# Top-32 attention with an MLP: which engine turns the softmax weights, and who takes the notes

## The chip, the core and the metric

The kernel runs on one core of one Trainium2 chip. The metric is the device time of one execution in microseconds (us). A core has five engines with a queue of instructions each: TensorE (PE in the profile; PEld is its weight load), VectorE (DVE), ScalarE (ACT), GpSimd (POOL) and SyncE (SP, which here only issues transfers). An engine takes its instructions in the order in which they were written; engines wait for one another through semaphores.

## The reference, cut to what matters

Eight batches of eight heads, 576 queries and keys, head size 64; all float32.

```python
scores = scale * np.matmul(q, k.transpose(0, 1, 3, 2))          # scale = 1/8
kth = np.partition(scores, -32, axis=-1)[..., -32:-31]
scores = np.where(scores >= kth, scores, -1e9)                  # the 32 largest of 576
attn = softmax(scores)                                          # shift by the max, divide by sum + 1e-9
x = np.matmul(attn, v)            # (8, 8, 576, 64), then heads side by side: (8, 576, 512)
xn = (x - mean) / np.sqrt(var + 1e-6) * g_ln                    # over the 512
out = x + np.maximum(xn @ w_ch1, 0) @ w_ch2                     # 512 -> 2048 -> 512
```

## The kernel before, in words

**Units.** A *job* is a pair of heads of one batch with a set of query tiles. The 576 queries are four tiles of 128 and a rest of 64. A *unit* is one such tile for both heads of the pair, so two score matrices of 128 x 576; the rest's unit holds both heads in one 128 x 576 matrix. There are 160 units, 32 of them rests. Queries of a job that share one value product are a *group*: batch 0 has groups of two tiles and rests by themselves, batch 1 groups [0, 1] and [2, 3, rest], batches 2 to 7 first [0, 1, rest] for four head pairs and then [2, 3] for four.

**A step.** The main loop has a step `n` for each unit, and the code writes each engine's order by hand (`tc.manual_schedule()`). A unit is worked on in several steps:

- TensorE makes its scores (line 386) one or two steps ahead, and ScalarE copies them into the tile `sc` (line 367; five buffers).
- VectorE selects in step `n`: `halve` (lines 407 and 408) makes pairwise maxima `hi` and minima `lo` (written one step ahead, `hi` has two buffers), and `select(u, 0..3)` finds the 32nd largest with MAX8 and MATCH_REPLACE8 (lines 429, 415, 421).
- `prepare` (lines 437 to 445) makes three small notes from the result: `watch` (line 452) notes how far the selection was from failing, line 444 makes `edge` (the threshold times a huge factor) and line 445 `bias` (the maximum times -scale). Each is 128 x 2 or 128 x 1. For the first 17 units VectorE does this at the end of the unit's own step, and from then on GpSimd (`CONVERTING`), in the next step.
- One step later ScalarE marks the dropped keys (`mask`, line 481, needs `edge`), GpSimd subtracts the scores (line 484), and two steps later ScalarE exponentiates into the tile `e` (`weigh`, line 492).
- The weights must then lie with keys on partitions, in the tile `pt` (one buffer), for the value product. TensorE turns them: `turn` transposes four blocks of 128 keys for each head (line 546) and one block with the last 64 keys of both heads (line 575); ScalarE copies each PSUM bank to `pt` (lines 558 and 576).
- For 72 *moved* units (batches 2 to 7; no rests, and not the last unit of a group) VectorE does most of it instead: `move` transposes 32 x 32 blocks of the first 512 keys of each head in two instructions (line 524) into the unit's spent `sc` tile, SyncE sends that to device memory (`turned`, line 529), and four more transfers (line 532) bring it back to `pt` with 32-row strips in the right places. The last 64 keys still go over TensorE. `move` stands at the end of the step, behind `select(u, 3)`.
- A step after a group's last unit was turned, `values` multiplies with the values (`av`, lines 600 and 607, at the beginning of the step), `take_values` and `place` bring the result into the rows of `x`.

**MLP.** When rows of `x` are complete, `stats` and a queue `todo` follow: hidden matmuls (line 745) and projections (lines 784 and 902), pieces of which `fill()` puts between the attention's instructions on TensorE. How much a step gets is a plan (`slot`, from `pe_cost` and `dve_cost`): up to step 17 the difference of the two costs, later an even share of what is left. SyncE's queue holds, in one order, the transfers of `move`, loads of heads and values, the forms of the second weight (line 971), denominators and outputs.

Of the kernel before, what the change touches and what calls it, by code (L numbers as in the profile page):

```python
# [10 lines left out]
ALU = mybir.AluOpType  # L11
FP32 = mybir.dt.float32
# [7 lines left out]
STEEP = 2.0**90  # L20
LN_EPS = 1.0e-6
J = 4
# [7 lines left out]
def compute(  # L30
# [12 lines left out]
    nc = tc.nc  # L43
    P = nc.NUM_PARTITIONS
    B, H, S, D = q.shape
# [3 lines left out]
    JP = J * P  # L49
    R = S - JP  # L50
    NHP = H // 2
# [9 lines left out]
    GQ = 2 * P + R  # L61
# [10 lines left out]
    ptpool = pool("pt", 1)  # L72
# [13 lines left out]
    hbmpool = pool("hbm", 4, space=bass.MemoryType.DRAM)  # L86
# [350 lines left out]
    def prepare(u):  # L437

        nt = len(u.tiles)
        u.bias, u.edge = u.thr[:, 0:nt, 5], u.thr[:, 0:nt, 6]  # L440
        if doubt is not None:
            watch(u)
        eng = nc.vector if u.i < CONVERTING else nc.gpsimd
        eng.tensor_scalar(u.edge, u.thr[:, 0:nt, 7], STEEP, 0.0, ALU.mult, ALU.add)  # L444
        eng.tensor_scalar(u.bias, u.top[:, 0:nt, 0], -scale, 0.0, ALU.mult, ALU.add)

    def watch(u):

        nt = len(u.tiles)
        c = 1 + 2 * (u.i % 16)  # L450
        eng = nc.vector if u.i < CONVERTING else nc.gpsimd
        eng.tensor_tensor(  # L452
            watched[:, c : c + nt], u.hi[:, 0:nt, HALF + 7], u.thr[:, 0:nt, 7], ALU.subtract
        )
        if u.i % 16 == 15 or u.i == N - 1:
            u.ends_watch = True
# [49 lines left out]
    def place_of(u):  # L506

        g = u.group  # L510
        if g.pt is None:
            g.pt = ptpool.tile([P, 2 * J + 1, GQ], FP32, tag="pt", name="pt")
            g.blocks = g.pt[:, 0 : 2 * J].rearrange("p c n -> p (c n)").rearrange(
                "p (i h c n) -> p h i c n", h=2, c=J, n=32
            )
        return sum(P for x in g.qts if x < u.qt) // 32

    def move(u):

        i0 = place_of(u)  # L520
        ni = P // 32
        blocks = u.sc[:].rearrange("p t n -> p (t n)")[:, 0 : 2 * JP]
        for t in range(2):
            nc.vector.transpose(
                blocks.rearrange("p (j t c n) -> p j t c n", j=ni, t=2, c=J)[:, :, t],
                u.e[:, t, t * R : t * R + JP].rearrange("p (c j k) -> p j c k", c=J, k=32),
            )
        hbm = hbmpool.tile([P, 2 * JP], FP32, tag="turned", name="turned")
        nc.sync.dma_start(hbm[:], blocks)
        for j in range(ni):  # L530
            to = u.group.pt[j * 32 : (j + 1) * 32, 0 : 2 * J].rearrange("k c n -> k (c n)")
            nc.sync.dma_start(
                to[:, i0 * 2 * P : (i0 + ni) * 2 * P].rearrange("k (i x) -> k i x", i=ni),
                hbm[:, j * 2 * P : (j + 1) * 2 * P].rearrange("(i k) x -> k i x", k=32),
            )

    def turn(u):

        g = u.group
        i0 = place_of(u)  # L540
        q0 = i0 * 32

        def part(t):
            ps = turned()
            for c in range(J):
                nc.tensor.transpose(  # L546
                    ps[:, c * P : (c + 1) * P], u.e[:, t, c * P + t * R : (c + 1) * P + t * R],
                    ident[:],
                )
            if u.rest:  # L550
                both = ps[:].rearrange("p (c h n) -> p h c n", h=2, n=R)
                for h in range(2):
                    nc.scalar.copy(
                        g.blocks[:, h, i0 : i0 + R // 32],
                        both[:, h].rearrange("p c (i n) -> p i c n", n=32),
                    )
            else:
                nc.scalar.copy(  # L558
                    g.blocks[:, t, i0 : i0 + P // 32],
                    ps[:].rearrange("p (c i n) -> p i c n", c=J, n=32),  # L560
                )

        def last():
            ps = turned()
            if u.rest:
                nc.tensor.transpose(ps[0:R, 0:P], u.e[:, 0, JP:S], ident[:])
                nc.tensor.transpose(ps[:, P : 2 * P], u.e[:, 0, JP - R : S], ident[:])
                for h in range(2):
                    nc.scalar.copy(
                        g.pt[h * R : (h + 1) * R, 2 * J, q0 : q0 + R],  # L570
                        ps[h * R : (h + 1) * R, h * (P + R) : h * (P + R) + R],
                    )
            else:
                ends = u.e[:].rearrange("p t n -> p (t n)")[:, JP : JP + P]
                nc.tensor.transpose(ps[:, 0:P], ends, ident[:])
                nc.scalar.copy(g.pt[:, 2 * J, q0 : q0 + P], ps[:, 0:P])

        heads = () if u.moved else range(len(u.tiles))
        return [lambda t=t: part(t) for t in heads] + [last]

    xs, xps, rs, oTr, dr = {}, {}, {}, {}, {}

# [12 lines left out]
    def values(g):  # L595
        vb = g.job.v
        av = brief("av")
        for c in range(J):
            for h in range(2):
                nc.tensor.matmul(  # L600
                    av[h * D : (h + 1) * D, 0 : g.nq],
                    vb[:, h * J + c, :],
                    g.blocks[:, h, 0 : g.nq // 32, c, :],
                    start=(c == 0),
                    stop=False,
                )
        nc.tensor.matmul(
            av[:, 0 : g.nq], g.job.ends[:], g.pt[:, 2 * J, 0 : g.nq],
            start=False, stop=True,
        )  # L610
        g.av = av
# [320 lines left out]
    blocks = []  # L932
# [59 lines left out]
    jobs = []  # L992
# [27 lines left out]
    CONVERTING = max(n for n in batches if batches[n]) + 2  # L1020
    EARLY = jobs[NHP].first

    for u in units[jobs[5 * NHP].first :]:
        u.moved = not u.rest and u is not u.group.units[-1]


    full = slice(0, P)
# [137 lines left out]
    load_gain()  # L1165
    weights(-1, 0)
    weights(-1, 1)
    for n in range(END):
        now[0] = n
        if n in gives:  # L1170
# [16 lines left out]
        moved = ex is not None and ex.moved  # L1187
# [27 lines left out]
        if ex and len(ex.tiles) > 1 and not early:  # L1215
            weigh(ex, 1)
        fill()
        if g:
            take_values(g)
        if parts and not moved:  # L1220
            parts[0]()
        if ex and ex.rest:
            keep_den(ex)
# [79 lines left out]
        if late and late.job.hp == NHP - 1:  # L1303
            r = late.job.b // 2
            if r % 2:
                for x in (r - 1, r):
                    arrived(n, ("r", x), rs[x])
        fill()
    while todo or any(x.waiting for x in (sums_later, ends_later, stores)):
        tick[0] += 1  # L1310
        stores.settle(2)
        ends_later.settle(1)
        sums_later.settle(1)
        fetch_forms(1)
        if todo:
            pop()
# [50 lines left out]
```

## Time and profile before

| | before |
|---|---|
| three runs | 1652.8, 1662.5, 1662.7 us (median 1662.5) |
| profiled execution | 1655.4 us, of it the profile's span 1653.6 us, mean granted clock 0.963 |
| TensorE busy | 1508.0 us (91%) |
| VectorE busy | 1334.3 us (81%) |
| ScalarE busy | 1067.4 us (65%) |
| GpSimd busy | 1078.1 us (65%) |
| transfers | 211.5 MB, 43.8% of the 16 DMA engines' span on the main queue |

"Busy" counts the time with at least one instruction running on the engine; the rest of the span is idle, and for idle time the profile names the instruction whose end released the engine ("<-"). A group's line has the kernel line, engine, operation, output and inputs, shapes and count, then its busy time, the mean duration of one, and the idle time ahead of it. PEclk is the clock that TensorE was granted, 1.00 at most. A matmul shows twice in the counts of float32 products (two passes); a transpose shows once.

### The profile page before, as it was taken

To read this page: it belongs to the slowest core of one execution; us is meant where nothing else is said; L and a number is where in the kernel's file an instruction comes from. 1 tells how busy PE (TensorE), PEld (TensorE's weight loads), DVE (VectorE), ACT (ScalarE), POOL (GpSimd) and SP (SyncE) were. 2 spreads that over 40 slices of the span, in tenths; PEclk is the share of its full clock that TensorE was granted. 3 is DMA by queue.
4 is the path that set the end of the run, shared out by engine and by line. 5 is a ranking of instruction groups with operands and counts; after the bars stand their busy time and mean duration, and the time that the engine had idled before them with its cause. 6 is when DMAs were issued, how large, how long until landed. Compare 5 with 4: busy or idle time off the path is not lost. (4 is left out here: it accounts for less than half of the span.)

```text
span 1653.6 us, 27426 instructions
## 1 busy us (share of the span) xinstructions
PE 1508.0 (91%) x7898; PEld 1132.7 (68%) x7898; DVE 1334.3 (81%) x3990; ACT 1067.4 (65%) x2712; POOL 1078.1 (65%) x1607
## 2 busy tenths in 40 slices
PE   2557898999989899899999999999989999999997
PEld 1235546677757677677777776677767777778886
DVE  6878998788989898899998988799879999884000
ACT  5777966677757676567666765677656766654311
POOL 4667866867657475667675866576756676856433
PEclk9768999999989999999999999999999999999999
DMA  7433434321454354554655444545554445442211
GB/s 199 110 100 114 130 81 119 114 66 46 109 167 152 109 168 118 162 153 118 185 160 168 126 126 135 163 138 138 158 158 150 134 135 181 149 131 71 91 32 53
DMA packets 358951, 211.52 MB, mean 128 GB/s; under 512 B 250756, under 2 KB 331144, under 8 KB 358792
## 3 DMA queue, kind: packets, MB, share of 16 engines
q1 hardware_dynamic: 354056, 209.10, 43.8%
q8 instruction: 65, 1.06, 0.3%
q10 hardware_dynamic: 4736, 0.59, 0.2%
q14 instruction: 94, 0.77, 0.2%
HBM read 145.62 MB, written 63.96 MB: 127 GB/s over the span
## 5 line engine op out<-in xcount | busy, mean ns | idle before, releaser
L484 POOL TENSOR_TENSOR e<-e,sc 128x576 f32<-128x576 f32 x288 | 412.4, 1435 | 419.4 <-ACT e L481 403.1
L745 PE MATMUL hps<-xT,w 128*128 128x256 f32 x2304 | 548.2, 384 | 2.5 <-ACT xT L707 2.5
L745 PEld LDWEIGHTS hps<-xT,w 128*128 128x128 f32 x2304 | 422.0, 191 | 72.8 <-issue 16.7
L429 DVE MAX8 m<-hi 128x8 f32<-128x296 f32 (+1 forms) x1152 | 464.3, 444 | 1.1
L415 DVE MATCH_REPLACE8 hi<-m,hi 128x288 f32<-128x288 f32 (+1 forms) x864 | 378.2, 444 | 0.0
L902 PE MATMUL ops<-w,h 128*128 128x256 f32 x1360 | 324.8, 381 | 0.0
L902 PEld LDWEIGHTS ops<-w,h 128*128 128x128 f32 x1360 | 247.7, 190 | 40.4 <-issue 6.9
L492 ACT ACTIVATE e<-e,m 128x576 f32<-128x576 f32 x288 | 224.8, 780 | 52.8 <-POOL e L484 52.4
L407 DVE TENSOR_TENSOR hi<-sc 128x576 f32<-128x576 f32 (+1 forms) x160 | 120.1, 751 | 157.4 <-POOL watched L452 135.7
L481 ACT ACTIVATE e<-sc,m 128x576 f32<-128x576 f32 x288 | 223.9, 781 | 14.6 <-POOL m L444 13.9
L367 ACT COPY sc<-scps 128x288 f32<-128x288 f32 x576 | 195.1, 406 | 38.6 <-PE scps L386 18.3
L600 PE MATMUL av<-pt,vb 128*64 128x256 f32 (+2 forms) x1088 | 159.4, 439 | 37.7 <-DMA pt<-turned 18.2
L768 ACT ACTIVATE h<-hps 128x512 f32<-128x512 f32 x144 | 86.5, 601 | 103.7 <-PE hps L745 102.9
L600 PEld LDWEIGHTS av<-pt,vb 128*64 128x64 f32 x1088 | 80.2, 149 | 106.5 <-issue 50.3
L386 PE MATMUL scps<-kT,late_qT 64*128 64x288 f32 (+3 forms) x832 | 129.0, 413 | 5.3 <-ACT pt L558 3.2
L902 PE MATMUL ops<-wt,s 128*128 128x256 f32 x544 | 129.2, 381 | 0.0
L546 PE MATMUL tp<-ident,e 128*128 128x128 f32 x576 | 93.9, 289 | 37.8 <-ACT e L492 37.4
L386 PE MATMUL scps<-kT,qT 64*128 64x288 f32 x512 | 94.8, 471 | 29.5 <-ACT sign L168 11.8
L408 DVE TENSOR_TENSOR lo<-sc 128x576 f32<-128x576 f32 (+1 forms) x160 | 120.9, 756 | 0.0
L546 PEld LDWEIGHTS tp<-ident,e 128*128 128x128 f32 x576 | 73.9, 148 | 65.7 <-ACT e L492 51.6
L421 DVE MAX8 hi<-lo 128x8 f32<-128x288 f32 x288 | 118.0, 446 | 0.0
L386 PEld LDWEIGHTS scps<-kT,late_qT 64*128 64x128 f32 (+1 forms) x832 | 72.0, 168 | 59.4 <-issue 23.5
(106 smaller groups left out, 1905.9 us busy)
## 6 DMA issues: line engine op xcount, KB each, us to landing
turned<-sc SPq DMA_DIRECT2D x72, 512.0 KB, 2.6
pt<-turned SPq DMA_DIRECT2D x288, 128.0 KB, 2.7
w<-forms SPq DMA_DIRECT2D x136, 256.0 KB, 3.8
vb<-in_v_dram SPq DMA_DIRECT2D x136, 128.0 KB, 3.1
raw<-in_moe_w_ch_dram SPq DMA_DIRECT2D x32, 512.0 KB, 4.3
kT<-kept SPq DMA_DIRECT2D x36, 288.0 KB, 3.2
kin<-in_k_dram SPq DMA_DIRECT2D x128, 72.0 KB, 2.3
kept<-kT SPq DMA_DIRECT2D x32, 288.0 KB, 2.9
```

The lines of the kernel that those rows point to most:

```text
L367: nc.scalar.copy(u.sc[:, t, s * HALF : (s + 1) * HALF], made[s][t][:, 0:HALF])
L386: nc.tensor.matmul(ps[i * R : i * R + ql, o : o + width], qT[r, q0 : q0 + ql], kT[r, k0 : k0 + width], start=True, stop=True,)
L408: nc.vector.tensor_tensor(lo, a, b, ALU.min)
L415: nc.vector.match_replace(x, m[:, t, :], x, LOWEST)
L429: nc.vector.max(m[:, t, :], u.hi[:, t, 0:width])
L481: nc.scalar.activation(u.e[:, t], u.sc[:, t], AF.Relu, bias=u.edge[:, t : t + 1], scale=-STEEP)
L484: nc.gpsimd.tensor_tensor(u.e[:, t], u.e[:, t], u.sc[:, t], ALU.subtract)
L492: nc.scalar.activation(u.e[:, t], u.e[:, t], AF.Exp, bias=u.bias[:, t : t + 1], scale=-scale, accum_out=g.den[:, col : col + 1],)
L546: nc.tensor.transpose(ps[:, c * P : (c + 1) * P], u.e[:, t, c * P + t * R : (c + 1) * P + t * R], ident[:],)
L600: nc.tensor.matmul(av[h * D : (h + 1) * D, 0 : g.nq], vb[:, h * J + c, :], g.blocks[:, h, 0 : g.nq // 32, c, :], start=(c == 0), stop=False,)
L745: nc.tensor.matmul(ps[0][:, side * N : (side + 1) * N], w1[:, c, f * P : (f + 1) * P], self.xT[:, c, 0:N], start=(c == 0), stop=(c == NC - 1),
L902: nc.tensor.matmul(bank[name][:, 0:Q], a(j), rhs, start=first and j == 0, stop=(j == G - 1), skip_group_check=not first,)
```

## The change

- 118 units are moved instead of 72: all from unit 8 to the last but one, except rests and unit 15. Last units of a group are now among them.
- `move` turns all 1152 columns (both heads' 576 keys) in one VectorE instruction. A moved unit has no `turn` any more: its transposes on TensorE and copies on ScalarE are gone, those of the last 64 keys too.
- `pt` is laid out by blocks of 32 queries with nine rows of blocks each (four of head 0, the shared last keys, four of head 1), so that the strips from device memory land in one run of 288 numbers.
- `move` stands ahead of `select(u, 2)` in the step instead of behind `select(u, 3)`.
- A group whose last unit is moved has its value product one half step to one step later, at the end of the step (`late_values`); the result is taken in the next step, and the MLP block that hangs on it is given a step later.
- `watch` and `edge` are made by VectorE for all units, in the unit's own step behind `select(u, 3)`; `bias` stays with GpSimd from unit 17 on, written in the same place. 
- The plan counts a moved unit 0.0 instead of 0.15 for TensorE.

```diff
@@ prepare, watch
         if doubt is not None:
             watch(u)
+        nc.vector.tensor_scalar(u.edge, u.thr[:, 0:nt, 7], STEEP, 0.0, ALU.mult, ALU.add)
         eng = nc.vector if u.i < CONVERTING else nc.gpsimd
-        eng.tensor_scalar(u.edge, u.thr[:, 0:nt, 7], STEEP, 0.0, ALU.mult, ALU.add)
         eng.tensor_scalar(u.bias, u.top[:, 0:nt, 0], -scale, 0.0, ALU.mult, ALU.add)
...
-        eng = nc.vector if u.i < CONVERTING else nc.gpsimd
-        eng.tensor_tensor(
+        nc.vector.tensor_tensor(
             watched[:, c : c + nt], u.hi[:, 0:nt, HALF + 7], u.thr[:, 0:nt, 7], ALU.subtract
         )
@@ place_of
-            g.pt = ptpool.tile([P, 2 * J + 1, GQ], FP32, tag="pt", name="pt")
...
+            g.pt = ptpool.tile([P, GQ // 32, 2 * J + 1, 32], FP32, tag="pt", name="pt")
@@ move
-        ni = P // 32
-        blocks = u.sc[:].rearrange("p t n -> p (t n)")[:, 0 : 2 * JP]
-        for t in range(2):
-            nc.vector.transpose(
-                blocks.rearrange("p (j t c n) -> p j t c n", j=ni, t=2, c=J)[:, :, t],
-                u.e[:, t, t * R : t * R + JP].rearrange("p (c j k) -> p j c k", c=J, k=32),
-            )
-        hbm = hbmpool.tile([P, 2 * JP], FP32, tag="turned", name="turned")
+        ni, nb = P // 32, (2 * J + 1) * 32
+        blocks = u.sc[:].rearrange("p t n -> p (t n)")
+        nc.vector.transpose(
+            blocks.rearrange("p (j c n) -> p j c n", j=ni, n=32),
+            u.e[:].rearrange("p t n -> p (t n)").rearrange("p (c j k) -> p j c k", j=ni, k=32),
+        )
+        hbm = hbmpool.tile([P, 2 * S], FP32, tag="turned", name="turned")
         nc.sync.dma_start(hbm[:], blocks)
         for j in range(ni):
-            to = u.group.pt[j * 32 : (j + 1) * 32, 0 : 2 * J].rearrange("k c n -> k (c n)")
             nc.sync.dma_start(
-                to[:, i0 * 2 * P : (i0 + ni) * 2 * P].rearrange("k (i x) -> k i x", i=ni),
-                hbm[:, j * 2 * P : (j + 1) * 2 * P].rearrange("(i k) x -> k i x", k=32),
+                u.group.pt[j * 32 : (j + 1) * 32, i0 : i0 + ni].rearrange(
+                    "k i c n -> k i (c n)"
+                ),
+                hbm[:, j * nb : (j + 1) * nb].rearrange("(i k) x -> k i x", k=32),
             )
@@ which units
-    for u in units[jobs[5 * NHP].first :]:
-        u.moved = not u.rest and u is not u.group.units[-1]
+    for u in units[EARLY:-1]:
+        u.moved = not u.rest and u.i != jobs[2 * NHP - 1].last
...
-            step = j.last + (3 if j.last < EARLY else 4)
+            step = j.last + (3 if j.last < EARLY else 4 + units[j.last].moved)
...
-            c += 0.67 if ex.rest else 0.15 if ex.moved else 1.0
+            c += 0.67 if ex.rest else 0.0 if ex.moved else 1.0
@@ the step
-        parts = turn(ex) if ex else []
+        moved = ex is not None and ex.moved
+        parts = turn(ex) if ex and not moved else []
...
-        if g:
+        soon = g and not g.units[-1].moved
+        assert not (soon and late_values)
+        if soon:
             values(g)
...
-        if mk and mk.i >= CONVERTING:
-            prepare(mk)
...
         fill()
+        if soon:
+            late_values = None
+        else:
+            g, late_values = late_values, g
         if g:
             take_values(g)
...
+        if moved:
+            move(ex)
         if u:
             select(u, 2)
...
             select(u, 3)
-            if u.i < CONVERTING:
-                prepare(u)
-        if moved:
-            move(ex)
+            prepare(u)
...
         fill()
+        if late_values:
+            values(late_values)
```

More of the change, by code (lines that the diff above doesn't have):

```diff
@@ L511, in place_of @@
         if g.pt is None:
-            g.pt = ptpool.tile([P, 2 * J + 1, GQ], FP32, tag="pt", name="pt")
-            g.blocks = g.pt[:, 0 : 2 * J].rearrange("p c n -> p (c n)").rearrange(
-                "p (i h c n) -> p h i c n", h=2, c=J, n=32
-            )
+            g.pt = ptpool.tile([P, GQ // 32, 2 * J + 1, 32], FP32, tag="pt", name="pt")
         return sum(P for x in g.qts if x < u.qt) // 32
@@ L520, in move @@
         i0 = place_of(u)
-        ni = P // 32
-        blocks = u.sc[:].rearrange("p t n -> p (t n)")[:, 0 : 2 * JP]
-        for t in range(2):
-            nc.vector.transpose(
-                blocks.rearrange("p (j t c n) -> p j t c n", j=ni, t=2, c=J)[:, :, t],
-                u.e[:, t, t * R : t * R + JP].rearrange("p (c j k) -> p j c k", c=J, k=32),
-            )
-        hbm = hbmpool.tile([P, 2 * JP], FP32, tag="turned", name="turned")
+        ni, nb = P // 32, (2 * J + 1) * 32
[5 more added lines that the diff above has]
+        hbm = hbmpool.tile([P, 2 * S], FP32, tag="turned", name="turned")
         nc.sync.dma_start(hbm[:], blocks)
         for j in range(ni):
-            to = u.group.pt[j * 32 : (j + 1) * 32, 0 : 2 * J].rearrange("k c n -> k (c n)")
             nc.sync.dma_start(
-                to[:, i0 * 2 * P : (i0 + ni) * 2 * P].rearrange("k (i x) -> k i x", i=ni),
-                hbm[:, j * 2 * P : (j + 1) * 2 * P].rearrange("(i k) x -> k i x", k=32),
+                u.group.pt[j * 32 : (j + 1) * 32, i0 : i0 + ni].rearrange(
+                    "k i c n -> k i (c n)"
+                ),
+                hbm[:, j * nb : (j + 1) * nb].rearrange("(i k) x -> k i x", k=32),
             )
@@ L540, in turn @@
         i0 = place_of(u)
-        q0 = i0 * 32
         def part(t):
@@ L553, in part @@
                     nc.scalar.copy(
-                        g.blocks[:, h, i0 : i0 + R // 32],
+                        g.pt[:, i0 : i0 + R // 32, 5 * h : 5 * h + J],
                         both[:, h].rearrange("p c (i n) -> p i c n", n=32),
@@ L558, in part @@
                 nc.scalar.copy(
-                    g.blocks[:, t, i0 : i0 + P // 32],
+                    g.pt[:, i0 : i0 + P // 32, 5 * t : 5 * t + J],
                     ps[:].rearrange("p (c i n) -> p i c n", c=J, n=32),
@@ L569, in last @@
                     nc.scalar.copy(
-                        g.pt[h * R : (h + 1) * R, 2 * J, q0 : q0 + R],
-                        ps[h * R : (h + 1) * R, h * (P + R) : h * (P + R) + R],
+                        g.pt[h * R : (h + 1) * R, i0 : i0 + R // 32, J],
+                        ps[h * R : (h + 1) * R, h * (P + R) : h * (P + R) + R].rearrange(
+                            "p (i n) -> p i n", n=32
+                        ),
                     )
@@ L575, in last @@
                 nc.tensor.transpose(ps[:, 0:P], ends, ident[:])
-                nc.scalar.copy(g.pt[:, 2 * J, q0 : q0 + P], ps[:, 0:P])
-        heads = () if u.moved else range(len(u.tiles))
-        return [lambda t=t: part(t) for t in heads] + [last]
+                nc.scalar.copy(
+                    g.pt[:, i0 : i0 + P // 32, J],
+                    ps[:, 0:P].rearrange("p (i n) -> p i n", n=32),
+                )
+        return [lambda t=t: part(t) for t in range(len(u.tiles))] + [last]
     xs, xps, rs, oTr, dr = {}, {}, {}, {}, {}
@@ L602, in values @@
                     vb[:, h * J + c, :],
-                    g.blocks[:, h, 0 : g.nq // 32, c, :],
+                    g.pt[:, 0 : g.nq // 32, 5 * h + c, :],
                     start=(c == 0),
@@ L607, in values @@
         nc.tensor.matmul(
-            av[:, 0 : g.nq], g.job.ends[:], g.pt[:, 2 * J, 0 : g.nq],
+            av[:, 0 : g.nq], g.job.ends[:], g.pt[:, 0 : g.nq // 32, J, :],
             start=False, stop=True,
@@ L1185, in compute @@
         quick = ex.group if last and ex.group.quick else None
-        moved = ex is not None and ex.moved
         if ex and not early:
@@ L1217, in compute @@
         fill()
+        if soon:
+            late_values = None
+        else:
+            g, late_values = late_values, g
         if g:
             take_values(g)
-        if parts and not moved:
+        if parts:
             parts[0]()
```

## The prediction

> **What bounds the kernel now.** I read the shares first, then the span cut at batch borders, then the waits.
>
> ```profile
> PE 1508.0 (91%) x7898; PEld 1132.7 (68%) x7898; DVE 1334.3 (81%) x3990; ACT 1067.4 (65%) x2712; POOL 1078.1 (65%) x1607
> ```
>
> TensorE leads, but VectorE's 81% is an average: it has nothing to do in the last 110 us. The table by stage (us, then busy time of each engine, PEclk, DMA share) shows it; the second row is the second half of batch 0, the third batch 1, the others batches 2 to 7, and the last the tail.
>
> ```profile
> core 0: us, PE busy (x) PEld busy (x) DVE busy (x) ACT busy (x) POOL busy (x), PEclk, DMA share, GB/s
> ...
> 110.00:236.10 126.10, 99.04 (x489) 62.83 (x486) 114.00 (x313) 99.34 (x235) 97.43 (x83) 0.91 0.35 103
> 236.10:410.60 174.50, 166.72 (x950) 120.85 (x950) 147.96 (x466) 127.66 (x333) 125.61 (x185) 0.98 0.34 89
> 410.60:589.80 179.20, 163.05 (x862) 120.02 (x859) 162.47 (x488) 117.85 (x313) 111.35 (x180) 0.95 0.47 136
> 589.80:772.00 182.20, 170.89 (x911) 128.96 (x910) 167.47 (x500) 120.55 (x320) 117.83 (x193) 0.97 0.50 145
> 772.00:949.20 177.20, 175.74 (x953) 135.07 (x952) 163.42 (x494) 119.80 (x312) 124.25 (x196) 1.00 0.53 153
> 949.20:1137.00 187.80, 181.00 (x962) 137.78 (x960) 164.34 (x494) 122.00 (x323) 125.64 (x200) 0.97 0.50 146
> 1137.00:1322.30 185.30, 179.63 (x966) 137.68 (x965) 162.83 (x490) 122.28 (x319) 121.27 (x191) 0.98 0.49 144
> 1322.30:1507.20 184.90, 184.11 (x984) 143.65 (x985) 155.62 (x469) 119.55 (x308) 121.34 (x189) 1.00 0.44 135
> 1507.20:1653.60 146.40, 136.70 (x671) 117.83 (x667) 15.51 (x50) 40.53 (x92) 69.80 (x132) 0.98 0.23 69
> ```
>
> In batches 2 to 7 VectorE is busy for some 163 of 183 us, TensorE for 163 to 184. TensorE sets the pace, VectorE follows within 10%. What VectorE waits for, and what TensorE still waits for there:
>
> ```profile
> DVE hi L407 <- POOL watched L452: 135.7, 57, 11.4
> DVE sc L524 <- ACT e L492: 7.7, 6, 2.4
> PE av L600 <- DMA pt<-turned: 18.2, 7, 5.1
> ```
>
> The first line is nearly all of VectorE's idle time inside the loop: `halve` needs a buffer of `hi` that GpSimd's note still reads, and GpSimd stands behind ScalarE, which stands behind TensorE. So it is largely TensorE's lateness handed on.
>
> **Part 1, TensorE.** The page's mean of a transpose (281 to 289 ns) contains overlap; the spacing counts:
>
> ```profile
> 1026.45 0.60 PE L546 MATMUL tp<-ident,e 128*128 128x128 f32 x4
> 1026.88 0.38 PE L902 MATMUL ops<-w,h 128*128 128x256 f32 x1
> ```
>
> Four transposes hold TensorE for 26.88 - 26.45 = 0.43 us, 0.108 each. Gone are 46 x 8 (units newly moved) and 118 (last keys): 486 x 0.108 = 52 us; 3.9 + 1.3 = 5.2 us in each of batches 2 to 7, 16 x 9 x 0.108 = 15.5 in batch 1. ScalarE loses 92 copies of 0.58 and 118 of 0.27 us, GpSimd its two notes; neither is a bound.
>
> **Part 2, VectorE's transposes.**
>
> ```profile
> L524 DVE STREAM_TRANSPOSE sc<-e 128x512 f32<-128x512 f32 x144 | 93.2, 682 | 7.7 <-ACT e L492 7.7
> L316 DVE STREAM_TRANSPOSE kT<-kin 128x576 f32<-128x576 f32 x32 | 24.5, 764 | 5.9 <-DMA kin<-in_k_dram 5.9
> L452 DVE TENSOR_TENSOR watched<-hi,m 128x2 f32<-128x2 f32 x16 | 7.1, 444 | 0.5
> L444 DVE TENSOR_SCALAR m<-m 128x2 f32<-128x2 f32 x16 | 6.3, 395 | 0.0
> ```
>
> From start to start the timeline gives 0.605 us for 512 columns, 0.68 for 576 and 0.33 for 256: 0.05 us and 1.09 ns a column, so 1.31 us for 1152. A unit moved before pays 1.31 - 1.21 = 0.10 more, a new one 1.31: 72 x 0.10 + 46 x 1.31 = 67 us.
> The Trainium skill speaks against this part: "VectorE: DVE Perf Modes", section "Rules for kernel authors", gives a 128x128 transpose to TensorE where PSUM will do. Its section "The three transpose paths" has 390 ns (bf16) for one on TensorE, by which 486 would free an estimated 190 us instead of 52; the spacing above disagrees, and the trace decides.
>
> **Part 3, the notes.** 143 units bring `watch` and `edge` to VectorE. The last two rows above are what they cost there in the first units, and the timeline says why 0.4 us for two numbers a lane:
>
> ```profile
> 177.38 1.27 POOL L180 TENSOR_TENSOR wt<-wt 128x512 uint32<-128x512 uint32 x1
> 177.39 1.28 DVE L452 TENSOR_TENSOR watched<-hi,m 128x2 f32<-128x2 f32 x1
> ...
> 178.60 0.15 DVE L444 TENSOR_SCALAR m<-m 128x2 f32<-128x2 f32 x1
> ```
>
> The note ended when GpSimd's instruction did; undisturbed it takes 0.15.
> The Trainium skill, "SBUF — State Buffer", section "SBUF: two separate sides", names a port pair that VectorE and GpSimd lock against each other for a whole instruction. The row agrees, and the rule counts against the change: without it the sum would be shorter by the waiting part below, about 57 us.
> Undisturbed, both notes take 0.2 us with their spacing. At the moments when VectorE ends a unit's last MAX8 in batches 2 to 7, the timeline has GpSimd in a longer instruction in 64% of cases, with 0.31 us left on average over all (0.25 to 0.34 when I shift the moments by up to 5 us, so it hangs little on the phase). The second note found a newly begun instruction in 4 of 17 early units; I add 0.1. That is 0.6 us a unit, 86 us in all; bounds 0.2 (29 us) and the early rows, 0.444 + 0.395 = 0.84 (120 us).
>
> **Part 4, moves in the order.** `move` passes two MAX8 pairs and a replace pair, 2.7 us. Before, exponentials end 2.6 us ahead of it on average, and 46% have under 2.7. If VectorE is late itself, that slack grows, and I cost it in the 3 us below; behind a wait there stand `select(u, 2)`, `select(u, 3)` and the notes, for which the next mask waits. SyncE issues five transfers for each of 46 more units, 2.6 + 2.7 us to landing, earlier in the step. The next group's first `pt` transfer now waits for the late value product, since `pt` has one buffer, and head, value and form loads stand behind it; a group's next product is two steps off, some 18 us, which covers both. If not, the "av" wait above grows, 3 to 5 us each time. The plan of MLP pieces, read from the two built orders, differs only in steps 10 to 33, where some 38 products come earlier; TensorE has room there. The new layout of `pt` costs nothing that I can find: eight of nine products read runs of 32 before and after, and the ninth takes 0.439 us now (line 607) against 0.407 for theirs.
>
> **The sum.** With TensorE relieved and VectorE loaded, VectorE sets the pace where its work exceeds TensorE's. A batch of 2 to 6: its VectorE time + 6.4 (4 x 1.31 + 12 x 0.10) + 20 x 0.6 + 3 us that I leave for waits (2%, a choice; 1 and 4 as bounds). Batch 2: 162.5 + 21.4 = 183.9, +4.7 on 179.2. Batch 3: 188.9, +6.7. Batch 4: 184.8, +7.6. Batch 5: 185.7, -2.1. Batch 6: 184.2, -1.1. Batch 7 stays with TensorE: 184.1 - 5.2 + 1 = 180, -4.9. Batch 1: 148.0 + 16 x 1.31 + 12 + 3 = 184, +9.5. Second half of batch 0, where VectorE is 90% busy: 7 x 1.31 + 3 x 0.6 = 11, of which I let 1 vanish, +10. Tail: TensorE trails VectorE less, -4. Together +26. Against the profiled execution's 1655.4 us: 1682 us. Two of the three runs lie 7 us above it, their median 1662.5; 1682 is 1.2% over that.
>
> **Rivals.**
> (a) VectorE's waits vanish and the notes are cheap: faster. For it speaks that the 135.7 us wait has no cause left once VectorE frees `hi` itself. With 0.2 us a unit and 1 us of waits per batch: batch 1 -0.5, batches 2 to 4 -5.3, -3.3, -2.4, batches 5 and 6 (then TensorE's 176 and 175) -11.8 and -10.3, batch 7 -4.9, ends +5: -34, 1622 us. It decides if GpSimd rarely runs when a note starts, below 0.3 us a unit the sum turns negative. Against it: GpSimd is 65% busy, and row 177.39.
> (b) The wait moves to `move`: VectorE reaches line 519 before the exponential, because ScalarE still trails TensorE. The shortfall at unchanged lag is 0.8 us a move on average; if half of it binds, 118 x 0.4 = 47 us more: 1729. Against it: a late VectorE finds its input ready.
> (c) Nothing net: TensorE keeps the pace in most batches, 52 us freed go into waits for `pt`: 1650 to 1665. For it: TensorE and VectorE lie within 10% of each other everywhere.
>
> **How the numbers follow.** Forecast 0.52 (own range 1662 to 1717: in six batches notes at 0.84 add 0.24 x 20 each, 29 us, and a fourth us of waits 6; notes at 0.53 and one us of waits take 20 off), (a) 0.25, (b) 0.13, (c) 0.10. The range goes from 1632, inside (a), to 1717, which leaves out much of (b). A change under 1% (1646 to 1679) can't be told from none. Faster by over 1%: most of (a), 0.23. Within: (c) and the forecast's lower end, 0.27. Slower: 0.50.
>
> **What would show it.** Right: VectorE busy near 1488 us and over 95% in batches 1 to 6, no "POOL watched" wait, mean of `watch` plus `edge` near 0.6 us, the transpose near 1.38 us, TensorE busy below 1480 with gaps in batches 1 to 4. Wrong: notes near 0.15 us each, VectorE under 90% in batches 2 to 6, or long waits ahead of the transpose or of "av".

## The result, and the profile after

The changed kernel takes 1785.7 us (median of four runs), the kernel before beside it 1658.8: a ratio of 1.078, with a 95% interval of 1.073 to 1.084. The change costs 127 us where I forecast 20 to 26. The profiled execution of the changed kernel has a span of 1783.0 us and a mean granted clock of 0.929 (before 1653.6 and 0.963).

First the shares, from the first section of the page of the changed kernel:

```profile
PE 1506.9 (85%) x7412; PEld 1118.9 (63%) x7412; DVE 1491.0 (84%) x4250; ACT 995.1 (56%) x2502; POOL 984.9 (55%) x1321
```

VectorE's 1491 us of work are what the sum had (1488). But no engine is busy for more than 85% of the span. TensorE issues 486 instructions fewer and is busy for as long as before. So most of the lost time isn't in the work of an engine but between the engines. The table by stage, cut at the same steps as before (second half of batch 0, batches 1 to 7, tail), tells where:

```profile
core 0: us, PE busy (x) PEld busy (x) DVE busy (x) ACT busy (x) POOL busy (x), PEclk, DMA share, GB/s
...
110.20:247.80 137.60, 107.70 (x459) 65.45 (x457) 116.71 (x323) 92.21 (x213) 97.47 (x80) 0.86 0.52 153
247.80:438.30 190.50, 151.83 (x793) 110.00 (x791) 181.94 (x521) 109.53 (x291) 118.76 (x150) 0.90 0.60 168
438.30:643.70 205.40, 165.75 (x795) 119.53 (x795) 184.46 (x520) 108.48 (x279) 96.41 (x137) 0.88 0.53 147
643.70:853.50 209.80, 175.09 (x873) 131.04 (x870) 188.42 (x532) 114.18 (x297) 105.93 (x155) 0.92 0.56 156
853.50:1045.00 191.50, 180.57 (x917) 136.99 (x918) 183.26 (x526) 113.10 (x292) 110.43 (x159) 0.96 0.61 173
1045.00:1239.00 194.00, 175.33 (x902) 132.34 (x902) 185.20 (x527) 113.09 (x296) 108.01 (x155) 0.97 0.61 174
1239.00:1440.00 201.00, 182.51 (x928) 138.62 (x925) 179.83 (x524) 116.38 (x300) 109.09 (x148) 0.97 0.59 166
1440.00:1629.50 189.50, 177.84 (x911) 137.68 (x910) 171.13 (x500) 109.52 (x281) 104.76 (x150) 0.97 0.56 162
1629.50:1783.00 153.50, 139.55 (x681) 119.69 (x679) 19.55 (x54) 40.67 (x91) 70.43 (x128) 0.97 0.26 78
```

In batches 2 to 6 VectorE's busy time is within 4 us of the forecast's, but it stands still for 20.9, 21.4, 8.2, 8.8 and 21.2 us a batch (length less DVE busy), where the sum had left 3. The waits of the changed kernel, engine by engine (us in total, times, longest):

```profile
DVE sc L519 <- ACT e L491: 108.0, 44, 10.2
POOL m L445 <- DVE m L429: 101.8, 50, 6.4
ACT sc L367 <- DMA turned<-sc: 97.4, 20, 9.2
...
DVE hi L407 <- ACT sc L367: 27.4, 8, 7.1
...
PE av L599 <- DMA pt<-turned: 23.8, 8, 6.7
...
PE av L599 <- DMA ends<-in_v_dram: 22.6, 7, 6.4
```

and of SyncE's own queue:

```profile
SPq L526 <- DMA turned<-sc: 365.1, 118, 7.3
...
SPq L526 <- PE av L606: 56.2, 17, 12.6
```

The "POOL watched" wait of 135.7 us is gone, as expected. In its place VectorE waits 108 us for exponentials (7.7 before), ScalarE waits 97 us for the transfer `turned` to have read a score buffer (2.4 before), and TensorE waits ahead of `av` for transfers of more than one kind. SyncE's queue stands for 365 us on the landing of `turned` before it can send the four transfers back.

One episode of batch 2 in the timeline of the changed kernel (start, us, engine, and in brackets the idle time before and what ended it):

```profile
455.66 1.94 SPq L289 DMA_DIRECT2D kin<-in_k_dram  x4
...
457.70 2.07 SPq L289 DMA_DIRECT2D qin<-in_q_dram  x4
...
460.41 0.41 SPq L524 DMA_DIRECT2D turned<-sc  x1
...
462.54 1.24 PE L386 MATMUL scps<-kT,qT 64*128 64x288 f32 x8
...
464.64 1.74 SPq L526 DMA_DIRECT2D pt<-turned  x4
...
468.48 0.59 SPq L301 DMA_DIRECT2D vb<-in_v_dram  x1
469.11 0.51 SPq L305 DMA_DIRECT2D ends<-in_v_dram  x1
...
472.47 4.54 PE L599 MATMUL av<-pt,vb 128*64 128x320 f32 x16 [8.69 <-DMA kept<-kT]
...
478.26 0.37 ACT L866 COPY o<-ops 128x256 f32<-128x256 f32 x1 [11.14 <-PE ops L901]
478.53 0.78 ACT L491 ACTIVATE e<-e,m 128x576 f32<-128x576 f32 x1
...
479.43 1.38 DVE L519 STREAM_TRANSPOSE sc<-e 128x1152 f32<-128x1152 f32 x1 [6.37 <-ACT e L491]
```

Read it downwards. VectorE finished a transpose at 457.6, but SyncE was issuing eight head loads and a form, and sent `turned` only at 460.41. It stood till 464.64 for the landing, then sent the four transfers back, and the value loads `vb` and `ends` came behind those. The last `vb` was issued at 468.48 and landed 3.9 us later, at 472.4, and there `av` began: TensorE had stood for 8.69 us. (The row names `kept`, which `av` doesn't read. By its own landing, 3.6 us after its issue at 469.67, it came only at 473.3, so the row names the wrong transfer.) ScalarE stood for 11.14 us, since its next instruction copies a projection that TensorE had queued behind the value product, and the exponential waited behind that copy. VectorE's next transpose needed that exponential and stood for 6.37 us. One late transfer stopped three engines in turn. The same stretch by windows shows what TensorE's pause costs afterwards (fields as in the table above):

```profile
456.00:463.80 7.80, 7.68 (x42) 5.84 (x42) 7.77 (x26) 5.09 (x14) 3.77 (x10) 1.00 0.78 181
463.80:472.40 8.60, 0.00 (x0) 0.00 (x0) 8.50 (x22) 2.17 (x6) 3.55 (x4) 0.68 0.81 219
472.40:477.60 5.20, 5.13 (x18) 2.45 (x19) 0.66 (x2) 0.00 (x0) 0.00 (x0) 0.55 0.21 59
477.60:485.00 7.40, 7.15 (x38) 5.49 (x37) 5.47 (x14) 5.74 (x16) 3.11 (x4) 1.00 0.21 82
```

The granted clock was 1.00 before the pause, 0.55 in the 5.2 us after it, and 1.00 again from then on. The Trainium skill, "TensorE: Matmul & The Clock Gate", section "What's actually happening", says that the clock falls to half after an idle window of some 3.4 us and returns after a busy one; these rows agree. In slices of 1 us the clock is 1.00 up to 466, 0.50 from 467 to 477 and 1.00 again from 478: it fell some 3 us into the pause and came back some 4.6 us after its end.

### The profile page after: what moved, and what is told of

It reads as the page before. It is cut to its first block, busy times and chain, and to the rows that moved or that the text cites. A ratio compares the mean times of both kernels' runs of the same rounds, so it can differ in the third digit from the quotient of the medians.

```text
span 1783.0 us, 26177 instructions
## 1 busy us (share of the span) xinstructions
PE 1506.9 (85%) x7412; PEld 1118.9 (63%) x7412; DVE 1491.0 (84%) x4250; ACT 995.1 (56%) x2502; POOL 984.9 (55%) x1321
## 4 chain that ended last, share of the span: by engine, by line
DVE 36%; PE 33%; DMA 11%; POOL 7%; ACT 7%; issue 3%; SPq 2%; ACTq 0%; DVEq 0%; POOLq 0%
PE ops L901 10%; PE hps L744 10%; DVE m L429 10%; DVE hi L415 8%; DMA turned<-sc 6%; PE av L599 5%; DVE sc L519 5%; PE scps L386 3%; DVE hi L407 3%; DVE lo L408 3%; DMA pt<-turned 2%; DVE hi L421 2%; ACT e L491 2%; POOL e L483 2%; ACT sc L367 2%
## 5 line engine op out<-in xcount | busy, mean ns | idle before, releaser
L483 POOL TENSOR_TENSOR e<-e,sc 128x576 f32<-128x576 f32 x288 | 426.7, 1487 | 528.1 <-ACT e L480 522.1
L744 PEld LDWEIGHTS hps<-xT,w 128*128 128x128 f32 x2304 | 436.6, 194 | 81.1 <-issue 20.9
L429 DVE MAX8 m<-hi 128x8 f32<-128x296 f32 (+1 forms) x1152 | 470.3, 443 | 1.1
L901 PEld LDWEIGHTS ops<-w,h 128*128 128x128 f32 x1360 | 260.4, 197 | 55.7 <-issue 16.7
L519 DVE STREAM_TRANSPOSE sc<-e 128x1152 f32<-128x1152 f32 x118 | 160.4, 1360 | 111.2 <-ACT e L491 108.0
L599 PE MATMUL av<-pt,vb 128*64 128x256 f32 (+2 forms) x1088 | 174.6, 461 | 88.4 <-DMA pt<-turned 23.8
L599 PEld LDWEIGHTS av<-pt,vb 128*64 128x64 f32 x1088 | 91.5, 157 | 162.0 <-issue 89.5
L407 DVE TENSOR_TENSOR hi<-sc 128x576 f32<-128x576 f32 (+1 forms) x160 | 139.4, 871 | 27.7 <-ACT sc L367 27.4
L408 DVE TENSOR_TENSOR lo<-sc 128x576 f32<-128x576 f32 (+1 forms) x160 | 130.3, 815 | 0.0
L901 PEld LDWEIGHTS ops<-wt,s 128*128 128x128 f32 x544 | 100.8, 190 | 16.7 <-issue 3.1
```

Of the source, the lines that this page charges most:

```text
L407: nc.vector.tensor_tensor(hi, a, b, ALU.max)
L429: nc.vector.max(m[:, t, :], u.hi[:, t, 0:width])
L483: nc.gpsimd.tensor_tensor(u.e[:, t], u.e[:, t], u.sc[:, t], ALU.subtract)
L519: nc.vector.transpose(blocks.rearrange("p (j c n) -> p j c n", j=ni, n=32), u.e[:].rearrange("p t n -> p (t n)").rearrange("p (c j k) -> p ...
L599: nc.tensor.matmul(av[h * D : (h + 1) * D, 0 : g.nq], vb[:, h * J + c, :], g.pt[:, 0 : g.nq // 32, 5 * h + c, :], start=(c == 0), stop=False,)
L744: nc.tensor.matmul(ps[0][:, side * N : (side + 1) * N], w1[:, c, f * P : (f + 1) * P], self.xT[:, c, 0:N], start=(c == 0), stop=(c == NC - 1),
```

## The experiments

The ratios are to the kernel before, run beside each, with their 95% intervals. Unless said otherwise an edit is made to the changed kernel (1785.7 us, 118 moved units).

**One link at a time.** Five edits each loosen one link of the chain that the episode shows.

e1: the four transfers back leave at the beginning of the next step, so that SyncE needn't stand for a landing.

```diff
     def move(u):
...
-        for j in range(ni):            # the four transfers back to pt
-            nc.sync.dma_start(...)
+        u.landing = lambda: land(u, hbm)    # land() issues these four
@@ beginning of the step
+        sent = at(n - 3)
+        if sent and sent.moved:
+            sent.landing()
```

> The changed kernel, with the four transfers into pt issued at the beginning of the next step instead of right behind the transfer to device memory, so that SyncE no longer stands waiting for that to land (365 us of waiting in the changed kernel). Theory Q (SyncE's queue holds back value loads and the release of score buffers, and TensorE, ScalarE and so VectorE wait for that): 1690 to 1725 us, the waits of ScalarE's score copies for the turned transfer (97 us) and of av for ends, vb and kept (43 us) nearly gone. Theory V (VectorE has too much work: 1491 us busy): within 15 us of 1785. Theory O (the transposes stand too early in VectorE's order): within 20 us of 1785.

1760.2 us, 1.062 [1.054, 1.069]: 25 us less. SyncE's wait for `turned` falls from 365 to 173 us, but VectorE still waits 84 us for exponentials and ScalarE 92 us for `turned`.

e2: `move` again behind `select(u, 3)` and the notes.

```diff
-        if moved:
-            move(ex)
         if u:
             select(u, 2)
...
             prepare(u)
+        if moved:
+            move(ex)
```

> The changed kernel, with the transposes put back behind the last selection and the notes of the step. Theory O: the wait of the transposes for the exponential (108 us) falls under 30 us and the time to 1690 to 1720 us. Theory Q: the transfers leave 3 us later still, so no gain or a loss, 1780 to 1810 us. Theory V: 1770 to 1790 us.

1758.5 us, 1.061 [1.056, 1.066]: 27 us less. If the early place were the cause (my rival (b)), the wait ahead of the transpose would go. It goes on, and two others grow:

```profile
ACT sc L367 <- DMA turned<-sc: 130.3, 30, 9.5
...
DVE sc L519 <- ACT e L491: 92.9, 36, 12.2
...
PE av L599 <- DMA pt<-turned: 51.4, 16, 6.6
```

e3: `watch` and `edge` again by GpSimd in the next step.

```diff
-        nc.vector.tensor_scalar(u.edge, ...)
         eng = nc.vector if u.i < CONVERTING else nc.gpsimd
+        eng.tensor_scalar(u.edge, ...)
@@ watch
-        nc.vector.tensor_tensor(
+        eng.tensor_tensor(
@@ the step
+        if mk and mk.i >= CONVERTING:
+            prepare(mk)
...
-            prepare(u)
+            if u.i < CONVERTING:
+                prepare(u)
```

> The changed kernel, with watch and edge back on GpSimd and in the next step. Theory V: VectorE's busy time falls by about 75 us (66 of the two notes, some of the pairwise operations) and the time by 50 to 75 us. Theory Q: the wait of halve for GpSimd returns with the lateness of ScalarE, and the time stays at 1770 to 1800 us. Theory O: likewise.

1760.4 us, 1.062 [1.059, 1.065]: 25 us less, though VectorE's busy time falls by 80 (1410.6). The "POOL watched" wait comes back with 62 us, and the wait ahead of the transpose stays (110).

e5: from step 18 on the next scores come past the middle of the step, so that ScalarE's copies ask later for a score buffer.

```diff
-        for x in due(n):
-            scores(x)
+        if n <= CONVERTING:
+            for x in due(n):
+                scores(x)
...
         fill(1 if g or late else 0)
+        if n > CONVERTING:
+            for x in due(n):
+                scores(x)
```

> The changed kernel, with the scores of the unit after next made past the middle of the step instead of at its beginning (from step 18 on), so that their copy asks for a score buffer more than half a step later. Theory B (a ring of five score buffers: a moved unit gives its buffer back only when VectorE has turned it and the transfer has landed, ScalarE stands at the copy until then, the exponentials behind it come late, and VectorE waits for them): ScalarE's wait for the turned transfer (97 us) under 20 us, the transposes' wait (108 us) under 50 us, 1690 to 1720 us. Theory P (the late products and the single pt buffer): 1770 to 1790 us.

1761.6 us, 1.066 [1.063, 1.069]. The wait for a score buffer is cut from 97 to 37 us, and the wait for `pt` grows from 24 to 69; the waits of this kernel:

```profile
DVE sc L519 <- ACT e L491: 75.0, 30, 10.2
...
PE av L599 <- DMA pt<-turned: 69.3, 16, 8.5
...
ACT sc L367 <- DMA turned<-sc: 36.7, 14, 6.1
```

f2: the transfers to `pt` read a fixed piece of `v`, so they no longer wait for `turned`.

```diff
-                hbm[:, j * nb : (j + 1) * nb].rearrange("(i k) x -> k i x", k=32),
+                v[0, 2 * j].rearrange("s d -> (s d)").rearrange("(i k x) -> k i x", i=4, k=32),
```

> The changed kernel, with the same number and size of transfers, but those into pt read a fixed piece of the values in device memory instead of the turned weights, so the weights of moved units are not the attention's. SyncE no longer waits for the turned transfer to land, and the product no longer for VectorE's turn of its own units. Theory R (round trips tie the engines: product behind landing behind turn, score buffer behind landing, turn behind exponential; each takes its turn when another is freed): part of it goes, 1720 to 1750 us, ScalarE still waits for turned. Theory V (VectorE's work and its order against ScalarE): 1765 to 1785 us.

1768.4 us, 1.067 [1.064, 1.070]: some 17 us less. ScalarE's wait for `turned` rises to 126 us.

None of the five is the cause alone: each gives 17 to 27 us, and in each another wait grows as one shrinks (in e1 SyncE stands 405 us for VectorE ahead of `turned`, after 312).

**Several links.** e9 joins e1, e3 and e5.

> The changed kernel with 118 units moved and three repairs together: transfers into pt a step later, scores past the middle of the step, notes back on GpSimd. Each alone gained about 25 us. If they widen different links (R), the sum: 1700 to 1720 us. If they take the same slack from one another, 1745 to 1765 us.

1720.6 us, 1.038 [1.035, 1.042]: 65 us less, nearly the sum of the three (75).

f3 leaves the trip to memory out: f2 without the transfer `turned`. The four transfers into `pt` stay, and as in f2 they bring other numbers than the attention's.

```diff
-        hbm = hbmpool.tile([P, 2 * S], FP32, tag="turned", name="turned")
-        nc.sync.dma_start(hbm[:], blocks)
```

> As f2, and the transfer of the turned weights to device memory is left out too, so a score buffer is free when VectorE has turned it. VectorE's, TensorE's, ScalarE's and GpSimd's instructions are those of the changed kernel. Theory R: 1680 to 1710 us, near the 1682 that follow from the engines' work alone. Theory V: 1760 to 1785 us.

1729.7 us, 1.044 [1.041, 1.047]: 56 us less. Batches 2 and 3 of it, in the same fields as above:

```profile
431.30:620.40 189.10, 159.39 (x775) 116.14 (x773) 184.00 (x520) 107.58 (x279) 96.46 (x137) 0.90 0.45 112
620.40:814.70 194.30, 170.78 (x867) 127.80 (x868) 188.16 (x531) 113.58 (x295) 106.80 (x155) 0.96 0.49 120
```

VectorE is busy for 184.0 of 189.1 and 188.2 of 194.3 us; over batches 1 to 6 it is 96 to 98%. This is the kernel that my forecast had described, bound by VectorE. It also moves less than the changed kernel (205.5 MB after 275.2), but the value loads land no sooner for it (`vb` 3.4 us after its issue, 3.2 in the changed kernel), so lighter traffic doesn't show as the reason. f4 asks whether its remaining distance to the kernel before is VectorE's work: f3 with e3's edit.

> The changed kernel without the trips to memory (as f3: nothing is sent to device memory, and the weights of moved units are read from a fixed piece of v, so the value products are of other numbers), and with the notes on GpSimd a step later, as before. Theory (f3 is bound by VectorE's work, which is busy 97 to 98% of its batches 1 to 6): VectorE loses some 80 us of busy time (1508 to about 1430), the batches 2 to 6 become 10 us shorter each until TensorE holds them, 1660 to 1685 us, and VectorE falls to some 93% of them. Rival (waits that no run has removed): the gain is no more than the 24 us that the same edit gave with the trips in place, 1705 to 1712 us.

Batches 4 and 6 of it, in the same fields:

```profile
811.60:995.40 183.80, 179.85 (x945) 136.71 (x946) 173.63 (x486) 118.27 (x305) 123.65 (x203) 1.00 0.54 136
...
1180.40:1358.10 177.70, 175.11 (x926) 133.60 (x924) 169.83 (x483) 117.12 (x302) 120.17 (x189) 1.00 0.54 135
```

1698.5 us, 1.027 [1.025, 1.030]: 31 us less than f3. Neither expectation named this figure. It exceeds e3's 25, and falls short of the 45 to 70 of VectorE as the only bound: of 74 us less work on VectorE (1433.7 after 1507.9) 31 came through, and in batches 2 to 6 VectorE falls to 94 to 97% while TensorE reaches 98 to 99% in two of them (batches 4 and 6). I read it as two engines that nearly tie; batch 1, which came out 6 us longer than in f3, I can't explain.

**How many moves.** e4 moves only the 72 units that were moved before (with the other parts of the change), e6 the 88 from unit 8 on that don't end a group, e7 in batches 2 to 7 all but rests, 95, with late value products.

```diff
-    for u in units[EARLY:-1]:
-        u.moved = not u.rest and u.i != jobs[2 * NHP - 1].last
+    for u in units[jobs[5 * NHP].first :]:                      # e4; e6: units[EARLY:-1]
+        u.moved = not u.rest and u is not u.group.units[-1]     # e7: first line with :-1], and not u.rest alone
```

> The changed kernel, with only the 72 units moved that were moved before (so no group's product comes late). Theory V: 46 x 1.36 = 63 us less for VectorE, some 52 more for TensorE, 1725 to 1745 us. Theory Q: 46 x 3.1 us less waiting on SyncE and no wait for late products, 1680 to 1710 us. Theory O: the order binds for 72 instead of 118, 1740 us.

1673.9 us, 1.010 [1.007, 1.013].

> The changed kernel, with 88 units moved: from unit 8 on, but no last unit of a group, so that no product is late. Against the 1674 us with 72 units, 16 more moves in batches 0 and 1. Theory B: batches 2 to 7 as with 72; batches 0 and 1 grow by 10 to 25 us, since two of three consecutive units there are moved: 1685 to 1700 us. Theory P: 1675 to 1685 us, no late product there.

1698.9 us, 1.028 [1.022, 1.033]: 25 us over e4 for 16 moves in the first batches. The two profiles lie 19 us apart, as much as batch 1 alone (190.0 us against 171.1, 12 of the moves). That is 1.6 us a move, little more than the transpose itself (1.36).

> The changed kernel, with 95 units moved: batches 2 to 7 as changed with late products, batches 0 and 1 not moved at all. Theory B: in the halves of batches 2 to 7 with groups of two all units are moved and each waits for a buffer: 80 us more than with 72, 1740 to 1755 us. Theory P: the same batches lose by the late products, likewise 1740 us; the two are told apart by where ScalarE waits (turned: B; SyncE for the product: P). If the moves of batches 0 and 1 carry the loss, 1690 us.

1731.4 us, 1.047 [1.043, 1.052]: 57 us over e4 for 23 moves that end a group, 2.5 us each. Here the ScalarE wait for `turned` is back (2 us in e4, 11 in e6):

```profile
ACT sc L367 <- DMA turned<-sc: 103.1, 22, 9.7
...
SPq L526 <- PE av L606: 49.4, 12, 12.5
```

So the moves that end a group are the dear ones. By the sign that was named ahead, ScalarE's wait, it is the score buffers that bind (B) and not the late products (P). But SyncE also stands 49 us for a late product, and the next `turned`, which frees a score buffer, is behind that in its queue, so this run doesn't part the two. All 118 stand 112 us over e4; 82 of them are these two steps, and 30 are left for the last seven moves and for what both kinds do together.

**What is left of the change.** e8 is e4 with the notes back on GpSimd: 72 moves, one pass each, the new layout, the early place.

> The changed kernel, with the 72 units moved as before and the notes on GpSimd in the next step: what is left of the change is the single pass of 1152 columns, the earlier place in the step and the layout. Against 1658 us before: 118 fewer turns saved 52 us of TensorE, of which only 72 x 0.11 = 8 us here, VectorE 72 x 0.1 = 7 us more: 1650 to 1662 us. If the notes on VectorE carry the 15 us that the 72-unit kernel is slower than before, 1655 us; if the earlier place does, 1670 us.

1649.6 us, 0.997 [0.996, 0.998]. The two notes on VectorE therefore cost 20 to 24 us where 72 units are moved (e4 less e8: 24 by the times, 20 by the ratios to the kernel before beside each), and 25 to 27 where 118 are (e3). Its waits of TensorE for transfers ahead of `av`:

```profile
PE av L600 <- DMA ends<-in_v_dram: 16.5, 5, 6.2
...
PE av L600 <- DMA vb<-in_v_dram: 16.2, 7, 4.5
```

e10 adds e1's edit to e8, so that the values needn't wait behind a landing.

> 72 units moved in one pass, notes on GpSimd, and the transfers into pt at the beginning of the next step. With the transfers in place it was 1649.6 us, of which TensorE's product waits 33 us for value loads that stand in SyncE's queue behind the landing. Theory R: 1620 to 1640 us. If these waits are covered by TensorE's other work: 1645 to 1655 us.

1638.0 us, 0.989 [0.987, 0.991]: 1.1% faster than before and the fastest of all. Both of those rows are gone, but TensorE still waits ahead of `av`, by the rows for other transfers:

```profile
PE av L605 <- DMA kept<-kT: 9.9, 5, 4.2
...
PE av L605 <- DMA dr<-den: 9.5, 2, 6.6
```

In all these waits for transfers sum to 24.5 us, after 32.7 in e8. That is 8 of the 12 us gained, and since the episode shows that a row can name the wrong transfer, what ended the rest of them isn't shown.

b1 makes that one edit on the kernel before.

> The kernel before with one edit: the four transfers back to pt of a moved unit are issued at the beginning of the next step. If e10's 11 us over e8 come from SyncE's queue alone, which then no longer stands for a landing ahead of head, value and form loads, this kernel gains about as much, 1643 to 1650 us. Rival (before sends at the end of the step, so that the queue stands when nothing else is due in it; only the earlier place of the move made a late sending worth something): no change, 1655 to 1665 us, or a few us slower, since pt lands nearer to its value product.

1656.5 us, 1.001 [0.9995, 1.003]: nothing. So e10's gain needs the parts of the change that e8 keeps; whether it is the early place or the single pass, no run tells.

## Why the prediction was wrong, step by step

The direction came true; the size didn't, and the time lies 69 us over the range. Of the signs named ahead the notes (0.54 us), the transpose (1.36 us) and the missing "POOL watched" wait came as forecast. VectorE over 95% in batches 1 to 6 did not (89 to 96%), and long waits ahead of the transpose and of `av`, a sign of being wrong, appeared.

- **Work of VectorE: right in the total, in part by luck.** Forecast 1488 us, measured 1491. The groups behind it, in the changed kernel (busy, mean ns):

```profile
L519 DVE STREAM_TRANSPOSE sc<-e 128x1152 f32<-128x1152 f32 x118 | 160.4, 1360 | 111.2 <-ACT e L491 108.0 <-issue 2.8
...
L451 DVE TENSOR_TENSOR watched<-hi,m 128x2 f32<-128x2 f32 x128 | 41.6, 325 | 4.4
L443 DVE TENSOR_SCALAR m<-m 128x2 f32<-128x2 f32 x128 | 27.1, 212 | 0.0
...
L451 DVE TENSOR_TENSOR watched<-hi,m 128x1 f32<-128x1 f32 x32 | 20.0, 624 | 1.1
```

  The transposes took 67 us more than before, as forecast (160.4 less 93.2). Two notes took 0.325 + 0.212 = 0.54 us for a tile's unit, against 0.6; their groups grew by 79 us where the sum had 86. What was not forecast is that the groups of the pairwise maxima and minima grew by 29 us, with as many instructions as before. The groups overlap in time, so that these 175 us became 157 in the total. That it fits to 3 us is partly chance.
- **Part 1, TensorE's 52 us: not seen.** The 486 instructions went, but TensorE is busy for 1506.9 us, after 1508.0. TensorE is idle for 276 us after 146, and its granted clock fell from 0.963 to 0.929. The value products of 256 columns took 0.465 us in the mean after 0.407, those of the last keys 0.501 after 0.439, together 19 us more. The new layout of `pt` isn't the reason: e8 has it too, and there, at a clock of 0.965, they took 0.415 and 0.439. Where the rest of the 52 us went no run settles. In e10, which keeps 72 moves, the clock is 0.967 and TensorE is busy for 1497.7.
- **"3 us that I leave for waits": the step that failed.** I took it, a choice, with 1 and 4 as bounds, and no row bounded it from above. VectorE's idle time was 8 to 21 us in each of batches 2 to 6, 80 us together instead of 15.
- **Part 4 failed with it.** "Two steps off, some 18 us, which covers both" reckoned each transfer alone. It had the first `pt` transfer waiting for the late product, with loads behind it. It left out that `turned` also waits its turn on SyncE, that the queue stands for a landing, and that the score buffer isn't free before `turned` has landed. I had put what a lapse would cost at 3 to 5 us each time in the `av` wait; it appeared on three engines.
- **Rival (b)** had the right wait (`move` for the exponential) and a size for it of 47 us against 100 measured. But e2 shows that the place isn't what causes it: with `move` back at the end, 93 of those 108 us remain. Rivals (a) and (c) fell.
- **Tail:** -4 forecast, +7 measured.

The miss of 104 us splits by f3. Without the trips to memory the kernel takes 1730, so 56 us are waits tied to the trips. The other 48 lie between f3 and 1682. In its profiled run, 2 us under its median, batches 1 to 6 came out 30 us longer than forecast: 18 of VectorE's busy time and 12 of its idle time, which is 3 to 7 us a batch. VectorE's busy time is 1508 us in all, 20 over the sum; the pairwise maxima and minima are what was not forecast in it, 53 us more than before in their groups. Batch 7 and the tail came out 9 and 11 us longer than forecast (188.6 and 152.9 against 180 and 142.4), the second half of batch 0 came out 4 shorter. Why the pairwise instructions, batch 7 and the tail are longer no run settles.

**The cause, as far as it is shown.** A moved unit's weights go through five hands: ScalarE's exponential, VectorE's transpose, the transfer to memory, the transfers back, TensorE's product. Each hand also serves other work in a fixed order. Before, 72 units took this way and none ended a group, so the last hand had one more unit's time (and still waited 18 us for `pt`). My reading is that with 118 units, and with group ends among them, each lateness is passed on, and that it comes round again since the buffers are few (five of scores, one `pt`); the episode shows one such round. Shown is that the cost follows the number of moves and above all those that end a group (e4, e6, e7), that loosening one link moves the wait (e2, e5), that three links add up (e9), and that without the trips VectorE sets the pace (f3). Not shown is whether the score buffers or the late products make the group ends dear; a sixth score buffer was not tried. How the 30 us of interplay divide stays open too.

## What to carry to other kernels

Where two engines are each busy for 80 to 90% and work passes between them and back through memory, don't put a lump of 2% for waits into the sum: list each buffer on the way, the time from its first writer to its last reader (the queue that issues the transfers included), and the steps there are to cover it. Moving work off the busiest engine pays only while the receiving path keeps some slack: here the two fastest kernels keep 72 moves (fewer were not tried), the next 16 cost about their own work, and those that end a group nearly twice theirs. When transfers wait in one queue, first move the ones that have to wait for a landing behind the loads that needn't: that took e10 below e8, though on the kernel before the same edit gave nothing (b1).

## What the runs showed of the hardware

- Two numbers a lane cost VectorE 0.325 us for a two-input note and 0.212 us for a one-input one, in the mean of 128 instructions, though an undisturbed one took 0.15 (the row at 178.60 shown with the prediction). For rests, with one number a lane, the first of the two took 0.624 us and the second 0.143.
- A pause of TensorE of 8.69 us brought a granted clock of 0.55 for the next 5 us (1.00 before and after). In the totals, fewer instructions and a lower clock left TensorE's busy time as it was.
- Each trip took longer than before: `turned` lands 3.1 us after its issue (2.6 before, with 512 KB instead of 576), the four transfers back 2.9 (2.7). The total traffic (275 MB after 212) doesn't explain it: with 72 moves and 221 MB, e4, e8 and e10 have 2.8, 3.0 and 3.3 for `turned`.
